# Another order of the same tasks in a fused recurrence and channel-mix kernel

## The chip, the cores and the metric

The kernel runs on one core of one Trainium2 chip. The metric is the device time of one execution in microseconds (us), as the median of three runs. A core has five engines with an instruction stream each: PE (matmul, with weight loads shown apart as PEld), DVE, ACT, POOL and SP, and 16 DMA engines that all queues share.

## The reference

A gated linear recurrence over 4 batches, 8 heads, 768 tokens and head size 48, whose output, as 384 channels per token, goes through a channel mix with 1024 hidden units:

```python
f = 1 / (1 + exp(-f_logit))
for t in range(S):
    state = f[:, :, t, :, None] * state + einsum('bhd,bhe->bhde', k[:, :, t], v[:, :, t])
    y[:, :, t] = einsum('bhd,bhde->bhe', q[:, :, t], state)
x = y.transpose(0, 2, 1, 3).reshape(B, S, H * D)
x_prev = concatenate([zeros((B, 1, D)), x[:, :-1, :]], axis=1)
xk = mu_k * x + (1 - mu_k) * x_prev
xr = mu_r * x + (1 - mu_r) * x_prev
k = maximum(xk @ w_k, 0)
return 1 / (1 + exp(-(xr @ w_r))) * (k * k @ w_v)
```

## The kernel before

**Work.** The recurrence is cut into 24 chunks i of 128 tokens (6 for each batch), the channel mix into 8 units u of 384 tokens (3 chunks). The mix's products are made as three products of high and low parts each (hi·hi, hi·lo, lo·hi), so that each weight and each operand is split in two by DVE, ACT and POOL.

**Tasks.** All work is cut into named tasks. For chunk i: loads `f`/`qk`/`v`; logarithms `zT`, `ez`, `ln`, `b`, `rb`, `e`; `q`, `kr`, `n`, `k`; `TR` or `QT` (transposes on PE) and `kt` (their copy, L363); `SP` (scores at L373 and sums at L393, on PE); `za`, `zb`, `T` (the state; `zb` is L330 or L333 on DVE); `YA`, `YB` (outputs, L410, on PE); `w`, `y` (copies), `bl` (L279) and `m` (the masked scores, L385). From chunk 8 on, `QT` `YA` `SP` `YB` of neighbouring chunks stand together as one bundle of small matmuls between the large ones. For unit u: `sp` (copies by DMA), `d`, `xm`, `xh`, `xl` (the mixed input and its two parts; `xh` is L544), `F` (L558, 9 matmuls each, input layer), `r`, `h`, `kk`, `l` (square and its parts), `R` (gate), `lg`, `sg` (sigmoid), `W` (output layer), `o` (L648, DVE), `out` (L652, the store; the last one goes out on ACT's queue, the others on SP's). The weights come in pieces: load, `S` L678, `T` L687, `X` L690 (all on DVE), `H` L693, `L` L697. `c`, `cm`, `lo`, `lot`, `lom` look at the inputs' sizes and set a flag, which `strong` (L802) reads into a register of every engine; at the end L887 branches around a general version of the whole program:

```python
at = U - 1
pl.add("lom", at, ("V", 0.6, 0, flag), uses=[("pm", "lo"), ("xm", "lo")])
pl.add("strong", at + 0.3, ("Q", 0.0, 0, load), after=["lom"])
...
k.emit(plan.schedule())
with tc.If(k.strong > 0):
    general(k, gen, out)
```

With the inputs timed here the flag is 0, the branch is taken on every engine, and the general code is skipped.

**What sets the order.** Two tables written out in full. `ORDER` lists every task once; `Plan.schedule` walks through it, a suffix (`:V` DVE, `:A` ACT, `:G` POOL) chooses the engine of a task, a token such as `+4y` puts four dummy matmuls (fillers, which keep PE running) there, and `HOMES` gives the buffer numbers. `Rwkv.emit` pins each engine's instructions to that order. So every engine works through its own part of `ORDER` strictly in turn, and waits where something that it needs from another engine or a DMA isn't there.

Of the kernel before, what the change touches and what calls it, by code (L numbers as in the profile page):

```python
# [63 lines left out]
+2m1 YA4 m4 d0.01 xh0.00:A xh0.02:A xm0.01 wvS3 xh0.01:V wvT3 wvX3 TR5 w4:A +1s YB4 kt5:A SP5 bl5:A wvH0 d0.12 za5:G
xl0.00:G xl0.02:G xl0.01:G d0.11 wvH3 wkH6 y4:A wvL0:G wkL6:G wvL3:G wkS5 F0.0 xm0.12 xm0.11 zb5 wkT5 wkX5 wkS7 wkT7 wkX7
F0.1 F0.2 YA5 F0.3 r0.0:A kk0.0:A d0.10 r0.1:A h0.0 h0.1 xm0.10 kk0.1:V m5 wv4 v8 v6 f3 wv5 b6 wvS4 wvT4 wvX4 r0.2:A l0.0:G
l0.1:G w5:A wkH5 YB5 kk0.2:A wkL5:G wrL3:G h0.2 ln6 rb6 r0.3:A kk0.3:A F0.4 F0.5 F0.6 r0.4:A wrH1 wkH7 h0.3 kr6:G l0.2:G
kk0.4:A r0.5:A h0.4 bl6:V q6 n6 k6 xh0.10:V xh0.12:V l0.3:V xh0.11:V xl0.10:V xl0.12:V TR6 kt6:A wkL7:G wrL1:G x01 F0.7 SP6
h0.5 kk0.5:A xl0.11:G l0.4:G l0.5:G r0.7:A y5:A wvH4 wvS5 wvT5 wvX5 r0.6:V kk0.6:V kk0.7:V h0.6 wvH5 R0.0 R0.1 R0.2 lg0.0:A
h0.7 b7 bl7:V m6 l0.7:V ln7 rb7 wvL4:G qk8 sp1.1 sp1.2 v7 sp1.0 l0.6:G wvL5:G kr7:G lg0.2:A lg0.1:A sg0 W0.00 W0.01 W0.10  # L70
W0.11 q7 n7 d1.1 k7 xm1.01 xm1.11 b8 d1.0 xm1.10 o0.0 xm1.00 ln8 rb8 bl8:A TR7 W0.20 W0.21 xh1.00:A kt7:A xh1.01:A xh1.10:A
xh1.11:A sf3 zb6:V T6 q8 kr8:G n8 k8 d1.2 out0.0 c5 qk9 xl1.00:G xl1.01:G xm1.02 xh1.02:A g7 xm1.12 o0.2 b9 QT8 YA6 w6:A SP7
YB6 ln9 rb9 xh1.12:A xl1.02:G za7:G xl1.10:G xl1.11:G kr9:G y6:A x02 g8 m7 q9 o0.1 F1.0 F1.1 F1.2 kt8:A qk10 zb7 bl9:V T7 n9
k9 za8:V b10 SP8 QT9 YA7 r1.0:A kk1.0:A h1.0 r1.2:A w7:A bl10:A ln10 rb10 kk1.2:V l1.0:G g9 m8 r1.1:V q10 zb8 kr10:G T8 n10
k10 h1.1 h1.2 kk1.1:A l1.2:V F1.3 YB7 v9 f4 qk11 out0.1 F1.4 F1.5 y7:A kt9:A b11 QT10 YA8 w8:V SP9 YB8 r1.4:A kk1.4:A h1.4
ln11 rb11 r1.5:V q11 bl11:V n11 l1.1:V za9:G xl1.12:G l1.4:G g10 g11 kr11:G k11 h1.5 kk1.5:A y8:A r1.3:A kk1.3:V l1.5:G h1.3
F1.6 F1.7 R1.0 R1.1 r1.6:V h1.6 r1.7:V h1.7 lg1.0:A kk1.6:A R1.2 l1.3:V kt10:V zb9 T9 m9 kk1.7:A za10:V cm5 lg1.1:A QT11 YA9
# [10 lines left out]
QT15 YA13 w13:V xl3.02:V SP14 YB13 za14:G bl16:A ln16 xh3.10:A rb16 kr16:G q16 cm2 n16 o2.2 zb14 k16 T14 m14 F3.0 F3.1 F3.2
F3.3 y13:A r3.0:A kk3.0:A h3.0 r3.1:A h3.1 kt15:A b17 xh3.12:V kk3.1:V v16 qk17 g15 l3.0:G za15:G xl3.10:V xl3.12:G l3.1:G
g16 QT16 YA14 w14:V SP15 YB14 r3.2:V r3.3:A xh3.11:A xl3.11:G ln17 rb17 kk3.3:A h3.3 h3.2 kk3.2:A zb15 bl17:V q17 y14:V F3.4  # L90
F3.5 F3.6 n17 l3.3:V m15 r3.5:V kr17:V kt16:V T15 k17 l3.2:G r3.4:A h3.4 kk3.4:A kk3.5:A h3.5 l3.4:G x04 l3.5:G r3.6:V F3.7
# [10 lines left out]
W4.11 W4.20 W4.21 v20 c9 out3.1 qk21 qk22 sf7 b21 ln21 bl21:A rb21 o4.0 out4.0 c13 b22 xh5.02:A ln22 rb22 bl22:A kr21:G q21
n21 k21 QT21 YA19 SP20 w19:A YB19 q22 o4.1 xl5.02:G g21 kr22:G kt21:A o4.2 xh5.11:V n22 k22 m20 b23 xh5.12:V zb20 T20 F5.0
F5.1 F5.2 r5.0:A y19:A h5.0 ln23 r5.1:V h5.1 QT22 YA20 kk5.0:V w20:V xl5.10:G xl5.11:G bl23:V cm13 cm9 l5.0:G SP21 YB20 v23
out4.2 qk23 out4.1 v22 rb23 r5.2:A kk5.1:A h5.2 y20:A kr23:G l5.1:G c8 sp6.0 sp6.2 q23 kk5.2:V F5.3 r5.3:A h5.3 kk5.3:A
l5.3:V l5.2:V n23 k23 kt22:V F5.4 F5.5 F5.6 r5.4:A h5.4 kk5.4:A g22 za21:G xl5.12:G g23 l5.4:G x06 r5.6:V m21 r5.5:V zb21
# [903 lines left out]
```

## Time and profile before

| | |
|---|---|
| time, median of 3 runs | 341.58 us (341.3 to 341.67) |
| time of the profiled execution | 341.73 us |
| its span, first to last instruction | 339.9 us |
| busy: PE, PEld, DVE, ACT, POOL | 320.8, 304.5, 255.5, 205.2, 153.4 us |
| matmuls | 4574 |
| moved by DMA | 45.24 MB |

Busy time is the sum of an engine's instructions as the profile shows them. The span's first part, up to the first `F` task (F0.0), is the start: loads, logarithms, weight pieces and the first chunks. The steady part follows, and the tail after the last matmul. PE's instructions are counted for the text as matmuls; each matmul has a weight load beside it, so 128 matmuls are 256 instructions, less a few waits that stand as instructions of their own.

### The profile page before, as it was taken

Reading aid. Unit: us, or ns where it says so; the run is one execution under the profiler, and the core shown is the slowest. Engines: PE = TensorE matmul, PEld = TensorE weight load, DVE = VectorE, ACT = ScalarE, POOL = GpSimd, SP = SyncE. Lnnn points to the kernel's source line nnn. Section 1 sums busy time; section 2 is a strip of 40 time slices with the busy share of each in tenths; the row PEclk is TensorE's granted clock in tenths of the full one; section 3 lists DMA queues with packets and bytes.
Section 4 is the critical chain, followed back from the end, with each engine's and each line's share of the span. In section 5 each row is a group of like instructions: output and inputs, shape, how many; then the busy total and the mean of one; then the engine's idle time right before and its main releaser. Section 6 shows DMA issues by size and latency. Waiting matters only on the chain. (4 is left out here: it accounts for less than half of the span.)

```text
span 339.9 us, 10992 instructions
## 1 busy us (share of the span) xinstructions
PE 320.8 (94%) x4574; PEld 304.5 (90%) x4574; DVE 255.5 (75%) x519; ACT 205.2 (60%) x432; POOL 153.4 (45%) x194
## 2 busy tenths in 40 slices
PE   4795889999999999999999999999999999999993
PEld 4675678899999999999999999999999999999993
DVE  5997999999988987686998886787475627837420
ACT  3888788784887736783658648591858236133420
POOL 2369589847762435313653356525612405214300
PEclk9999999999999999999999999999999999999999
DMA  7999667015465234470257122541520133040002
GB/s 230 398 385 360 185 193 273 14 29 158 175 198 152 75 97 153 102 267 25 87 125 269 62 46 85 170 143 60 187 91 5 32 117 92 35 141 23 0 4 79
DMA packets 20347, 45.24 MB, mean 133 GB/s; under 512 B 2752, under 2 KB 12736, under 8 KB 20288
## 3 DMA queue, kind: packets, MB, share of 16 engines
q1 hardware_dynamic: 20144, 44.25, 39.4%
q8 instruction: 38, 0.62, 0.8%
q10 hardware_dynamic: 144, 0.20, 0.2%
q14 instruction: 21, 0.17, 0.2%
HBM read 38.54 MB, written 4.72 MB: 127 GB/s over the span
## 5 line engine op out<-in xcount | busy, mean ns | idle before, releaser
L558 PE MATMUL pm<-xh,wk 128*128 128x384 f32 x384 | 103.5, 341 | 0.7 <-DVE words L690 0.5
L558 PE MATMUL pm<-wv,k2h 128*128 128x384 f32 x384 | 98.4, 338 | 0.0
L596 POOL TENSOR_TENSOR k2l<-kk,k2h 128x384 fp32r<-128x384 f32 x44 | 46.4, 1059 | 63.6 <-DVE kk L588 24.9
L558 PEld LDWEIGHTS pm<-xh,wk 128*128 128x128 f32 x384 | 69.8, 188 | 2.3 <-DVE words L690 0.6
L558 PEld LDWEIGHTS pm<-wv,k2h 128*128 128x128 f32 x384 | 69.0, 188 | 0.9 <-issue 0.5
L558 PE MATMUL pm<-wv,k2l 128*128 128x384 f32 x192 | 64.5, 336 | 0.4 <-issue 0.4
L558 PE MATMUL pm<-xl,wk 128*128 128x384 f32 x192 | 64.5, 336 | 0.0
L550 POOL TENSOR_TENSOR xl<-xm,xh 128x384 fp32r<-128x384 f32 x35 | 37.4, 1075 | 32.2 <-DVE xh L544 27.8
L289 POOL TENSOR_TENSOR qk<-qk,rb 128x256 f32<-128x256 f32 x23 | 17.1, 742 | 60.6 <-ACT rb L275 33.1
L586 ACT ACTIVATE k2h<-r 128x384 fp32r<-128x384 f32 x64 | 32.2, 519 | 12.8 <-DVE r L582 12.4
L558 PE MATMUL pm<-wr,xh 128*128 128x384 f32 x144 | 37.1, 339 | 0.3 <-DVE words L690 0.3
L558 PEld LDWEIGHTS pm<-wv,k2l 128*128 128x128 f32 x192 | 36.1, 188 | 0.0
L558 PEld LDWEIGHTS pm<-xl,wk 128*128 128x128 f32 x192 | 36.0, 188 | 0.0
L581 ACT ACTIVATE r<-pm 128x384 f32<-128x384 f32 x41 | 20.0, 488 | 24.5 <-PE pm L558 22.2
L558 PEld LDWEIGHTS pm<-wr,xh 128*128 128x128 f32 x144 | 25.8, 188 | 0.8 <-DVE words L690 0.6
L443 ACT ACTIVATE x<-py 64x128 f32<-64x128 f32 (+1 forms) x69 | 21.4, 310 | 8.1 <-PE py L410 4.9
L535 DVE SCALAR_TENSOR_TENSOR xm<-pm,mu_sb,x 128x384 f32<-128x384 f32 x42 | 24.9, 609 | 0.6
L270 DVE TENSOR_TENSOR_SCAN pm<-f,low 128x512 f32<-128x512 f32 x18 | 25.0, 1387 | 0.5 <-ACT f L624 0.3
L590 ACT ACTIVATE kk<-r 128x384 f32<-128x384 f32 x38 | 19.4, 519 | 9.6 <-DVE r L582 7.1
L558 PE MATMUL pm<-wr,xl 128*128 128x384 f32 x72 | 24.2, 336 | 0.0
L410 PE MATMUL py<-qk,z 64*64 64x64 f32 x704 | 21.6, 227 | 1.7 <-DVE z L330 0.9
L582 DVE TENSOR_SCALAR r<-pm 128x384 f32<-128x384 f32 x23 | 12.4, 549 | 12.8 <-PE pm L558 12.1
(129 smaller groups left out, 575.6 us busy)
## 6 DMA issues: line engine op xcount, KB each, us to landing
qk<-in_qkt SPq DMA_DIRECT2D x24, 512.0 KB, 5.6
...
v<-in_vt SPq DMA_DIRECT2D x24, 192.0 KB, 2.9
out<-o SPq DMA_DIRECT2D x23, 192.0 KB, 3.4
...
```

The lines of the kernel that those rows point to most:

```text
L270: pl.add(f"b{i}", ga, ("V", 1.25, 1, lambda: nc.vector.tensor_tensor_scan(b().rearrange(FL), f().rearrange(FL), self.low.rearrange(FL), 1. ...
L289: e.tensor_tensor(k()[:, ::2], k()[:, ::2], rb()[:, ::2], op=ALU.mult)
L410: first[c, h] = nc.tensor.matmul(to, lhs, rhs, start=(c, h) not in first, stop=stop, skip_group_check=True)
L443: e.activation(o, i_, AF.Copy, scale=sign)
L535: pl.add(f"xm{u}.{n}{j}", pr, ("V", 0.62, 0, lambda xm=xm, n=n, j=j: nc.vector.scalar_tensor_tensor(xm(), pm("d", u, j)[:, :UT], self.mu_s ...
L550: e.tensor_tensor(lo(), xm(), hi().bitcast(F32), op=ALU.subtract)
L558: nc.tensor.matmul(ps, lhs(a, j), rhs(bb, j), start=ends[0] and i == 0, stop=ends[1] and i == len(pr) - 1)
L581: pl.add(f"r{u}.{f}", kf, ("A", 0.5, 0, lambda r=r, ps=ps: nc.scalar.activation(r(), ps(), AF.Relu)), ("V", 0.56, 0, lambda r=r, ps=ps: nc ...
L582: ("V", 0.56, 0, lambda r=r, ps=ps: nc.vector.tensor_scalar(r(), ps(), 0.0, None, op0=ALU.max)),
L586: pl.add(f"h{u}.{f}", kf, ("A", 0.53, 0, lambda r=r, hi=hi: nc.scalar.activation(hi(), r(), AF.Square)), after=[f"r{u}.{f}"], **kw)
L590: ("A", 0.53, 0, lambda r=r, kk=kk: nc.scalar.activation(kk(), r(), AF.Square)),
L596: e.tensor_tensor(lo(), kk(), hi().bitcast(F32), op=ALU.subtract)
```

## The change

`ORDER` and `HOMES` are other tables; no task, no helper and no other line differs. The diff replaces all of both; here is its beginning and its end:

```diff
 ORDER = """
-f0.0 sf0.0 cst zT0 ez0 ln0 +2y b0 wr2 wrS2 wrT2 wrX2 wk2 wr0 wkS2 wrS0 f0.1 f0.2 sf0.1 wrT0 wkT2 sf0.2 wrX0 wkX2 wrH2 rb0
...
-TR3 w2:V YB2 e4 rb5 wrH3 bl4:A kt3:A wkH4 y2:A T2 wvS2 wvT2 wvX2 wrL2:G wkL3:G wkL2:G za3:G wkL4:G wkL0:G v3 SP3 x00 wk1 f2
...
-out6.1 c12 out6.2 lg7.0:A h7.7 l7.7:G W7.01 cm14 cm12 lg7.1:A lo lot W7.10 W7.11 lom strong lg7.2:V sg7 o7.0 out7.0 o7.1
-out7.1 W7.20 W7.21 o7.2 out7.2
...
+q3 T2 wvS2 +1m0 YA2 kr3:G x00 kr4:G wkL2:G za3:G TR3 w2:A wkH4 e4 kt3:A YB2 y2:A b5 SP3 wvT2 onemu wvX2 q4 bl4:V wvH2 rb5 e5
+wvS0 wvT0 f2 wr1 v4 zb3 T3 m3 TR4 kt4:A +4y SP4 YA3 wrS1 bl5:V wrT1 wrX1 wvX0 w3:V wk1 sf2 wvH0 m4 wkS1 wkT1 qk5 za4:G wkX1
...
+l7.5:G cm3 R7.2 W7.00 lo lg7.1:V lot lg7.2:A l7.6:G out6.0 sg7 kk7.7:V l7.7:G W7.01 W7.10 W7.11 W7.20 W7.21 o7.1 out7.1 o7.0
+o7.2 lom out7.2 strong out7.0
```

**DVE in the start, around `zb3` (L330, which waits for SP3's sums on PE).** Before, the piece `wvX2` (the first L690) and one more weight instruction stand ahead of it; `m` is L385, `T` is L336, `q` is L281:

```order
L678 TENSOR_SCALAR pm_94<-words_123 128x512
L687 SCALAR_TENSOR_TENSOR pm_94<-words_123,pm_94 128x512
L690 SCALAR_TENSOR_TENSOR words_123<-words_123,pm_94 128x512
L678 TENSOR_SCALAR pm_96<-words_k2h_131 128x384
L330 TENSOR_TENSOR z_77<-pss,z_76 128x4x48
L385 TENSOR_TENSOR ss_100<-pss,mask 128x512
L336 TENSOR_TENSOR sm<-pss,z_77 128x192
```

After the change the same place reads:

```order
L678 TENSOR_SCALAR pm_96<-words_123 128x512
L687 SCALAR_TENSOR_TENSOR pm_96<-words_123,pm_96 128x512
L775 TENSOR_SCALAR one_mu<-mu_sb 128x6
L690 SCALAR_TENSOR_TENSOR words_123<-words_123,pm_96 128x512
L281 TENSOR_TENSOR qk_64<-qk_64,pm_95 128x512
L279 COPY bl<-pm_95 128x4
L678 TENSOR_SCALAR pm_93<-words_122 128x512
L687 SCALAR_TENSOR_TENSOR pm_93<-words_122,pm_93 128x512
L330 TENSOR_TENSOR z_77<-pss,z_76 128x4x48
L336 TENSOR_TENSOR sm<-pss,z_77 128x192
L385 TENSOR_TENSOR ss_100<-pss,mask 128x512
```

`q4`, `bl4`, `wvS0` and `wvT0` have moved ahead of `zb3`.

**PE in unit 1, around the bundle of chunks 8 and 9.** Before, SP8 (L373, L393), QT9 (L351) and the first part of the L410 group (YA7) follow F1.2, the nine matmuls of F1.3 stand in between, and YB7 comes behind them:

```order
L373 MATMUL pss<-qk_64 64x64 x16
L393 MATMUL pss<-v_103,ktk_101 48x48 x16
L351 MATMUL py<-ident,qk_65 128x64 x8
L410 MATMUL py<-qk_67,z_77 64x64
L410 MATMUL py<-qk_67,z_76 64x64 x2
...
L558 MATMUL pm_96<-xh_124,wk_83 128x384
L558 MATMUL pm_96<-xl_125,wk_83 128x384
...
L410 MATMUL py<-qk_67,z_76 64x64
L410 MATMUL py<-ss_100,v_104 48x64 x16
```

After the change it is one bundle, directly behind F1.1 (the last of whose nine matmuls is the first row):

```order
L558 MATMUL pm_96<-xh_124,wk_84 128x384
L351 MATMUL py<-ident,qk_65 128x64 x8
L410 MATMUL py<-qk_67,z_77 64x64
L410 MATMUL py<-qk_67,z_76 64x64 x2
...
L373 MATMUL pss<-qk_64 64x64 x16
L393 MATMUL pss<-v_105,ktk_101 48x48 x16
L410 MATMUL py<-qk_67,z_76 64x64
...
L410 MATMUL py<-ss_100,v_104 48x64 x16
L558 MATMUL pm_93<-xh_124,wk_83 128x384
```

All 136 small matmuls of the bundle now stand together, one F task earlier.

**The end on SP.** The flag is loaded at L802; the `out` rows are stores of the last unit. Before:

```order
L652 DMA out<-o_119 128x384
L802 TENSOR_LOAD flag
L802 ISA x2
L652 DMA out<-o_120 128x384
L652 DMA out<-o_119 128x384
L887 COMPARE_AND_BRANCH
```

After:

```order
L652 DMA out<-o_120 128x384
L652 DMA out<-o_119 128x384
L802 TENSOR_LOAD flag
L802 ISA x2
L652 DMA out<-o_120 128x384
L887 COMPARE_AND_BRANCH
```

The load now has one store behind it instead of two. On DVE the four small instructions that make the flag (L795 to L798) have moved behind the last `o` (L648) and stand directly ahead of the branch:

```order
L648 TENSOR_TENSOR o_119<-pm_94,lg_121 128x384
L648 TENSOR_TENSOR o_120<-pm_93,lg_121 128x384
L648 TENSOR_TENSOR o_119<-pm_96,lg_121 128x384
L795 TENSOR_REDUCE xm_114<-pm_95 1x1
L796 TENSOR_REDUCE xm_114<-pm_95 1x1
L797 TENSOR_SCALAR xm_114<-xm_114 1x1
L798 SCALAR_TENSOR_TENSOR flag<-xm_114 1x1
L802 TENSOR_LOAD flag
L887 COMPARE_AND_BRANCH
```

Before, L795 to L802 stood ahead of `lg7.2` (L616) and of all three L648 rows.

## Rows read from the trace of the kernel before

**Rows 1.** Windows: length, busy (x instructions) of PE, PEld, DVE, ACT, POOL; clock; DMA; GB/s

```profile
27.25:33.45 6.20, 3.82 (x127) 3.27 (x126) 4.41 (x10) 4.73 (x13) 5.93 (x9) 1.00 0.94 366
45.50:81.90 36.40, 35.44 (x379) 33.43 (x381) 35.48 (x63) 27.86 (x58) 27.24 (x28) 1.00 0.38 124
45.50:112.40 66.90, 65.56 (x1016) 61.70 (x1017) 63.26 (x119) 51.09 (x108) 43.72 (x50) 1.00 0.45 144
112.40:334.40 222.00, 221.90 (x2830) 215.74 (x2829) 154.02 (x319) 119.96 (x252) 84.89 (x102) 1.00 0.30 95
```

**Rows 2.** Timeline of PE, its stops: start, duration, instruction, idle before

```profile
27.25 0.34 PE L373 MATMUL pss<-qk 64*64 64x64 f32 x8 [0.98 <-issue]
33.45 0.51 PE L373 MATMUL pss<-qk 64*64 64x64 f32 x19 [2.38 <-issue]
45.50 0.48 PE L410 MATMUL py<-ss,v 64*48 64x64 f32 x18 [0.58 <-issue]
47.16 0.44 PE L558 MATMUL pm<-xh,wk 128*128 128x384 f32 x1 [0.48 <-DVE words L690]
112.42 0.34 PE L558 MATMUL pm<-wv,k2l 128*128 128x384 f32 x1 [0.40 <-issue]
```

**Rows 3.** Waits in the start, 0 to 48 us: total, times, longest

```profile
DVE z L330 <- POOL qk L290: 2.0, 1, 2.0
DVE z L330 <- PE pss L393: 0.8, 1, 0.8
```

**Rows 4.** Windows of the start, columns as in group 1

```profile
9.00:35.00 26.00, 20.42 (x514) 16.78 (x515) 22.25 (x50) 22.16 (x51) 17.03 (x23) 1.00 0.97 368
35.00:47.20 12.20, 9.91 (x268) 7.90 (x267) 11.99 (x23) 9.12 (x21) 7.42 (x10) 1.00 0.69 220
```

**Rows 5.** Timeline of DVE in the start, single instructions

```profile
13.46 0.55 DVE L363 COPY ktk<-pm 128x384 f32<-128x384 f32 x1
16.57 0.35 DVE L333 COPY z<-pss 128x192 f32<-128x192 f32 x1
44.60 1.18 DVE L544 CAST xh<-xm 128x384 fp32r<-128x384 f32 x1
```

**Rows 6.** DMA view at 43.1, 82.0 and 110.1 us: packets, MB, busy share

```profile
q8 instruction: 1, 0.02, 60.3%
q8 instruction: 1, 0.02, 59.2%
q8 instruction: 1, 0.02, 60.4%
```

**Rows 7.** Windows, one bundle (QT11, YA9, SP10, YB9), columns as in group 1

```profile
107.01:109.31 2.30, 2.30 (x137) 2.15 (x136) 1.20 (x3) 2.16 (x3) 0.08 (x1) 1.00 0.72 223
```

**Rows 8.** Timeline of the end: the flag, the last output and its store

```profile
326.10 0.25 DVE L795 TENSOR_REDUCE xm<-pm 1x1 f32<-1x96 f32 x1 [5.79 <-PE pm L791]
326.64 0.15 DVE L798 SCALAR_TENSOR_TENSOR flag<-xm 1x1 int32<-1x1 f32 x1
334.92 0.56 DVE L648 TENSOR_TENSOR o<-pm,lg 128x384 f32<-128x384 f32 x1 [3.31 <-SPq L887]
335.51 0.38 ACTq L652 DMA_DIRECT2D out<-o  x1
```

**Rows 9.** SP's load of line 802: duration ns min/median/max, first and last start

```profile
L802 SPq TENSOR_LOAD <-flag x1: 477/477/477, 326.8 to 326.8; - x1
```

**Rows 10.** Instructions of line 887 on SP, columns as in group 9

```profile
L887 SPq EVENT_SEMAPHORE  x8: 17/17/17, 334.7 to 338.5; - x8
...
L887 SPq COMPARE_BRANCH  x1: 45/45/45, 332.0 to 332.0; - x1
```

**Rows 11.** Instructions of line 1006, columns as in group 9

```profile
L1006 SPq EVENT_SEMAPHORE  x10: 17/28/28, 338.6 to 339.9; - x10
```

**Rows 12.** DMA view 325 to 340 us: issues, KB each, us to landing

```profile
out<-o SPq DMA_DIRECT2D x2, 192.0 KB, 3.6
out<-o ACTq DMA_DIRECT2D x1, 192.0 KB, 2.7
```

More of the change, by code (lines that the diff above doesn't have):

```diff
@@ L60 @@
-e3 wkH3 w1:A bl3:A kt2:A m1 wrS3 wrT3 wrX3 T1 YB1 SP2 wk6 qk3 wv2 za2:G kr3:G wkH0 rb4 y1:A wkS6 wkT6 wkX6 zb2 m2 q3 b5 YA2
-TR3 w2:V YB2 e4 rb5 wrH3 bl4:A kt3:A wkH4 y2:A T2 wvS2 wvT2 wvX2 wrL2:G wkL3:G wkL2:G za3:G wkL4:G wkL0:G v3 SP3 x00 wk1 f2
-qk4 kr4:G wkS1 wv0 zb3 m3 T3 wkT1 wkX1 +1m1 YA3 +2s TR4 wr1 v4 qk5 wvH2 e5 sf2 w3:A wkH1 kt4:A q4 wvS0 wvT0 wrS1 wrT1 wrX1
-wvX0 q5 +4s YB3 wvL2:G za4:G kr5:G wkL1:G sp0.2 sp0.0 v5 sp0.1 d0.02 wv3 qk6 wk5 qk7 wk7 d0.00 xm0.02 y3:A xm0.00 SP4 zb4 T4
@@ L64 @@
[L64 to L77, printed above, removed]
@@ L88 @@
[L88 to L91, printed above, removed]
@@ L102 @@
[L102 to L106, printed above, removed]
@@ L117 @@
[L117 to L119 removed]
+cst f0.2 sf0.2 zT2 ez2 ln2 f0.0 sf0.0 zT0 ez0 ln0 f0.1 sf0.1 +1y zT1 wr2 wv1 wrS2 wrT2 wrX2 wrH2 ez1 ln1 b0 rb0 e0 wr0 qk0
+v0 wk2 qk1 wk0 wvS1 wvT1 wrS0 wrT0 wrX0 wvX1 b1 b2 wrH0 wvH1 kr0:G bl0:V q0 wkS2 wkT2 wkX2 rb1 e1 TR0 kt0:A +2y SP0 rb2 wkH2
@@ new lines @@
+e2 kr1:G TR1 f1 q1 wkS0 wkT0 wkX0 sf1 wk6 v1 zb0:A YA0 m0 bl1:A kt1:A zT3 T0 bl2:A w0:A wkH0 wkS6 wkT6 wkX6 mg0 wvL1:G za1:G
+zT5 SP1 YB0 ez3 ln3 ez5 y0:A wr3 qk2 wrS3 wrT3 m1 wrX3 zb1 T1 q2 wk3 v2 wk4 zT4 b3 YA1 w1:V kr2:G wrL0:G wkH6 wkL0:G wkL6:G
+za2:G TR2 YB1 ez4 ln4 kt2:A rb3 e3 wkS3 wkT3 wkX3 SP2 qk3 wkH3 y1:A b4 ln5 rb4 wkS4 wkT4 wkX4 zb2 m2 wv2 qk4 mu v3 wv0 bl3:V
+q3 T2 wvS2 +1m0 YA2 kr3:G x00 kr4:G wkL2:G za3:G TR3 w2:A wkH4 e4 kt3:A YB2 y2:A b5 SP3 wvT2 onemu wvX2 q4 bl4:V wvH2 rb5 e5
@@ new lines @@
+wvS0 wvT0 f2 wr1 v4 zb3 T3 m3 TR4 kt4:A +4y SP4 YA3 wrS1 bl5:V wrT1 wrX1 wvX0 w3:V wk1 sf2 wvH0 m4 wkS1 wkT1 qk5 za4:G wkX1
+zb4 q5 +1m2 YB3 wkL3:G wrL2:G wvL2:G sp0.0 d0.00 xm0.00 T4 xh0.00:V kr5:G wkL4:G wvL0:G y3:A TR5 sp0.1 sp0.2 d0.01 v5 wk7
+wv3 wk5 qk6 xm0.01 d0.02 wrH3 kt5:A YA4 w4:A +1m2 +2s SP5 YB4 xh0.01:A d0.11 xm0.02 wkS7 wkT7 wkX7 xm0.11 wvS3 wvT3 wvX3
+xh0.02:A d0.10 wkH1 wkH7 d0.12 y4:A wvH3 za5:G xl0.00:G xl0.01:G xl0.02:G x01 wkL1:G wrL3:G wvL3:G F0.0 F0.1 xm0.12 zb5
+xm0.10 wkS5 wkT5 wkX5 F0.2 YA5 F0.3 r0.0:A h0.0 kk0.0:A r0.1:A h0.1 kk0.1:A r0.2:A w5:A m5 b6 wv4 wv5 qk7 qk8 f3 v6 wkH5 YB5
@@ new lines @@
+xl1.00:G ln9 T6 q8 n8 k8 d1.2 xm1.02 xh1.10:A xh1.01:A rb9 xh1.02:A QT8 YA6 SP7 w6:A YB6 y6:A kt8:A bl9:V o0.1 q9 n9
+xl1.01:G g7 za7:V xl1.02:G g8 kr9:G zb7 T7 xm1.12 k9 m7 F1.0 F1.1 out0.0 c8 v10 qk10 b10 QT9 YA7 w7:V SP8 YB7 xh1.11:A
+r1.0:A h1.0 kk1.0:A ln10 rb10 bl10:A xh1.12:A za8:G xl1.10:G r1.1:V zb8 T8 o0.2 l1.0:G kr10:G m8 q10 n10 k10 kk1.1:A h1.1
+kt9:V l1.1:G F1.2 F1.3 r1.3:V F1.4 F1.5 y7:A r1.2:A kk1.2:A h1.2 r1.4:A h1.3 kk1.3:A b11 ln11 rb11 QT10 YA8 l1.2:V w8:V
+out0.2 v9 qk11 SP9 YB8 f4 v11 out0.1 l1.3:V xl1.12:G xl1.11:G g9 za9:G x02 h1.4 kk1.4:V l1.4:G kr11:G r1.5:A kk1.5:V kt10:V
```

96 lines of the change are left out of this document (54 added, 42 removed).

## The prediction

> **What bounds the kernel now.** I read the windows first, then what PE waits for, then DVE in the start, then the end. The windows [rows 1] show a PE that does not rest: from 112.40 to 334.40 it is busy 221.90 of 222.00 us, from 45.50 to 112.40 it is busy 65.56 of 66.90, and the granted clock is 1.00 in every row, which is the higher of the two levels. DVE is busy 154 of 222 us there and nothing waits for it long. So the time is three parts: how late PE comes to the first F task (F0.0, 47.16 us, [rows 2]), the steady matmuls, the same products in both kernels, and what follows the last matmul. Only waits that PE meets on the way can lengthen the middle part.
>
> PE's own stops are the next thing to see [rows 2]: 0.98 us before 27.25, 2.38 before 33.45, 0.58 before 45.50, 0.40 before 112.42. All four say "issue": no engine was waited for. They stand at fixed counts: 127 matmuls lie between the first two and 1016 = 8 x 127 between the last two [rows 1], that is 256 instructions with the weight loads. And in the DMA view an instruction packet of 16 KB on queue q8 starts 2.4 us before PE goes on at 45.50, at 43.1, and 2.3 us before 112.42, at 110.1 [rows 6]. I read this as PE's instructions being fetched in blocks of 256: a block is asked for some time after PE enters the one ahead of it, is there 2.35 us after its packet starts, and PE stops if it gets through a block sooner. The delay up to the packet varies. The three blocks from 45.50 on end at 81.9 (381 weight loads, [rows 1]) and the packet starts at 82.0, 0.1 us later. The block ahead of 112.42 begins inside the bundle of [rows 7], at 107.6 by counting back 127 matmuls, and its packet starts at 110.1, 2.5 us later. Over the 28 blocks from 45.50 on the middle delay is 0.7 us.
>
> DVE in the start is nearly full: 22.25 of 26.00 us, then 11.99 of 12.20 [rows 4]. Its two long waits are 2.0 and 0.8 us, both ahead of L330 (`zb3`, `zb2`) [rows 3]. The 2.0 is put down to POOL, whose instruction had ended long before; what came last were SP3's sums on PE, inside which the stop of 2.38 us stands. The 0.8 is the same with SP2 and the stop of 0.98. The transfers are heavy to 35 us too (share 0.97).
>
> **The change, part 1: the start.** I counted DVE's work in its order up to the last instruction that F0.0 needs. Before, that is `xh0.01`, with 75 tasks of 39.9 us in all. After, it is `xm0.02` with 73 tasks, 37.5 us by the same durations. Left out are `kt0` 0.55 and `zb0` 0.35, now on ACT, the 1.18 of `xh0.01` (stretched; its like take about 0.4) [rows 5], `wvS3`, `w0`, `w2` and two `bl`; five small copies and one `xh` come in. So 2.4 us go. Then the waits: the order shows `q4`, `bl4`, `wvS0` and `wvT0`, some 2.5 us by their durations, now ahead of `zb3`. They run while SP3 stands still, so at most the 2.0 us of [rows 3] are filled too. Together 4.4 us could go, but ACT carries the copies (22.16 of 26 us, hardly freer than DVE, [rows 4]), the transfers set when weights are there, and a stop just ahead of SP4 is possible (below). Walking through the new order by hand with these durations puts F0.0 at 43.5 to 45 us; I take 44.3, **-2.9**. Bounds: -1.2, half of the work that goes and no wait filled, and -4.2, nearly everything. Two fillers fewer (14 to 12) are in the walk. The DVE work between F0.0 and later F and R tasks is equal within 0.5 us, so I see nothing that takes this gain back in unit 0.
>
> **Part 2: the blocks of 256.** In the steady part the order of the matmuls moves where blocks end. Large matmuls take about 0.34 us busy each but one starts every 0.17 us, a block of them lasts 22 us; a bundle of 136 small ones takes 2.30 us [rows 7], so a block that falls on one bundle whole is through in little over 2 us. Before, the nearest pair of block ends is 3.6 us apart and passes without a stop; the only steady stop, 0.40, has 4.8 us but the latest packet of all. After, counting through the order: one block begins at the seventh matmul of F1.1, just ahead of the bundle in the order shown, and ends inside YB7, 2.4 us later; one runs from the end of F3.2 into YB14, 2.1 us; one from YA20 into F5.4, 2.2 us. W1.01 meets an end as before, 4.6 us. With a delay of 0.65 and 2.35 to arrive, a block needs 3.0 us: stops of 0.6, 0.9 and 0.8, together **+2.3**. Bounds: with no delay, or a block asked for ahead, +0.2; with the longest delay seen, 2.5 us, each stop is 2.5 to 2.8 and W1.01's is kept, and not all three can be the worst, so +5. I take the middle delay, since [rows 6] has both short and long ones. Joining SP8 and YB7 to one bundle saves a change between small and large matmuls, **-0.1**.
>
> The Trainium skill speaks against this term. "Runtime: NRT & Kernel Launch", section "Instruction fetch mechanics", also has refills in 16 KiB blocks of 256 instructions, but says that the cost of crossing is mostly hidden; by that the term would be 0 and the sum -1.0, 340.7 us. The four stops of [rows 2] do not agree with "hidden" for dense small matmuls, and the measurement decides.
>
> **Part 3: the tail.** Before, the flag is made from 326.10 to 326.79 [rows 8], 7 us ahead of the end; SP's load takes 0.477 [rows 9] and lies beside the last matmuls. SP's branch, taken, starts at 332.0 and its next instruction runs at 334.7 [rows 10]: 2.7 us to fetch the code behind the skipped part, hidden too. What ends last is the store of ACT, issued at 335.51 [rows 8], landing 2.7 later [rows 12], and ACT's own branch; then SP's events run from 338.6 to 339.9 [rows 11]. After, the order shows the four flag instructions behind the last `o`, which ends at 335.48 before [rows 8]. Counted on that clock: 0.69 for the flag, 336.2; SP's load 0.48, 336.7, and some 0.5 to move and check it; a store `out7.0` (0.4 to issue) that stands behind the load; the branch at 337.4; 2.7 to the next code, 340.1; then about the 1.3 us of [rows 11] and the eight events ahead of them [rows 10], some 0.5: 341.9. The store alone gives nearly the same: issued at 337.3, 2.7 to 3.6 to land [rows 12], and about 1.2 behind it, 341.2 to 342.1. Against 339.9 I take **+2.0**, bounds +1.4 (events overlap the landing) and +2.8 (both late and one after the other). What is queued behind the flag's load is each engine's branch; DVE's and ACT's (both ready by 337) end before SP's.
>
> By the skill's same section a taken branch to code outside the loaded window forces a fetch; the trace agrees, 2.7 us on SP.
>
> **Sum.** -2.9 + 2.3 - 0.1 + 2.0 = +1.3. The profiled execution took 341.73 us, 1.83 beyond its span of 339.9; it stands 0.15 above the median of the runs. Against the median 341.58 the sum gives **342.9 us**. A measurement of this kernel can tell about 0.2%, 0.7 us, from no change.
>
> **Rivals.**
> - *The blocks come in time* (other side). The mechanism is the same queue, but packets start as at 82.0, right at the crossing, and a block is there when the bundle ends; the stops add up to 0.2. Then -2.9 + 0.2 - 0.1 + 2.0 = -0.8, 340.8 us. For it: every steady block but one passed without a stop in the trace. Against it: none was shorter than 3.6 us, and a packet needs 2.35. It decides for faster where the three stops stay under 0.3 us in all. Chance 0.22; a start of -4.2 with stops of 1.2 together (-1.1, 340.5) ends on the same side and adds 0.03.
> - *The start's gain is absorbed.* SP4 now holds a block end only 3.9 us after the one in SP3, in the time when transfers are densest and packets come latest (3.5 us after the crossing for the one at 43.1); a stop of 2 us there, with `zb4` and what follows on DVE waiting for it as `zb3` did, leaves -0.5 to -1 of the start: -0.8 + 2.3 - 0.1 + 2.0 = +3.4, 345.0. For it: two of the four stops stood in just such places. Against it: DVE has other work ahead of most of its waits now. Chance 0.15.
> - *The terms cancel.* Stops of 0.3 to 1.5 us, or a start nearer -4, land within 0.7 us of before: 341.6. Chance 0.22.
> - *The forecast*, +0.7 to +2.6: 0.38.
>
> That the change does not do what it says is no rival: each engine's order is pinned.
>
> **Numbers.** Faster 0.25 (first rival and the large start), same 0.22, slower 0.53 (forecast and absorbed start). The range leaves out the fastest tenth (stops of nothing with a start beyond -3.4) and the slowest tenth: 340.3 to 344.9. The forecast alone covers 342.3 to 344.2.
>
> **What would show it.** F0.0 between 43.5 and 45 us shows part 1 right; 46 or later with an "issue" stop in SP4 shows the absorbed start. PE stops marked "issue" of 0.3 us or more inside YB7, YB14 and F5.4 show part 2 right, a steady part without them the first rival. The flag made behind the last `o`, SP's branch as the last long wait and 7 to 8 us from the last matmul to the end, against 5.6 before, show part 3. I am wrong if DVE or a transfer holds PE somewhere in the steady part, where I saw the same work in another order and took it as covered, or if the granted clock falls below 1.00.

## The result and the profile after

The changed kernel takes 346.0 us (median of 4 runs, 344.12 to 348.07); before, beside it, takes 341.62. The ratio is 1.0139, with a 95% interval of 1.0106 to 1.0172: slower by 3.6 to 5.9 us. It lies above the forecast of 342.9 and above its range. The second comparison of the same kernel (e1 below) gave 1.0097 (1.0064 to 1.013), 3.3 us; the four runs of the first were on the late side. In three of the kernels below (e4, e8, e10) one execution took 400 to 1079 us, which nothing here explains; the ratios do not contain them.

The profiled execution took 344.12 us, span 342.4. The windows, cut at F0.0 (47.94) and at the second R task of unit 0 (R0.1, 65.77), ahead of which PE waits for DVE for 0.2 to 0.3 us in all four profiles of the two kernels; columns as in [rows 1]:

```profile
9.00:47.94 38.94, 32.10 (x776) 26.31 (x775) 35.22 (x73) 32.46 (x72) 26.92 (x34) 0.91 0.86 309
47.94:65.77 17.83, 17.61 (x221) 16.31 (x213) 16.61 (x30) 15.41 (x38) 16.75 (x16) 1.00 0.45 159
65.77:334.40 268.63, 268.35 (x3565) 260.42 (x3565) 190.81 (x394) 156.42 (x320) 111.48 (x138) 1.00 0.33 103
```

PE is full behind R0.1, as it was. But F0.0 comes at 47.94 where it was 47.16 [rows 2], not at 44.3, and the clock, 1.00 in all rows before, is 0.91 in the start. The stops and waits of PE, timeline as in [rows 2], the last row of the steady part:

```profile
34.44 0.51 PE L373 MATMUL pss<-qk 64*64 64x64 f32 x19 [2.06 <-issue]
40.67 0.33 PE L344 MATMUL pm<-ident,qk 128*128 128x128 f32 x1 [0.29 <-POOL qk L289]
41.36 0.55 PE L344 MATMUL pm<-ident,qk 128*128 128x128 f32 x3 [0.36 <-POOL qk L290]
42.97 0.46 PE L410 MATMUL py<-qk,z 64*64 64x64 f32 x16 [1.06 <-ACT stage L443]
90.17 0.38 PE L410 MATMUL py<-ss,v 64*48 64x64 f32 x10 [0.23 <-issue]
```

The stop inside SP3 is there again. Two new waits stand behind it, on POOL (`kr5`, ahead of TR5) and on ACT (`y3`, ahead of YA4). The stop inside YB7 is exactly where it was forecast, but it is 0.23 us and not 0.6; inside YB14 and F5.4 there is none. And SP4's block end, which the absorbed-start rival named, passes without a stop.

The end, timeline and then lines 802, 887 and 1006 on SP, with PE's branch (PEldq), columns as in [rows 8] and [rows 9]:

```profile
334.01 0.34 PE L558 MATMUL pm<-wv,k2l 128*128 128x384 f32 x1
334.38 0.56 DVE L648 TENSOR_TENSOR o<-pm,lg 128x384 f32<-128x384 f32 x1 [3.08 <-PE pm L558]
334.86 0.23 DVE L795 TENSOR_REDUCE xm<-pm 1x1 f32<-1x96 f32 x1
335.39 0.15 DVE L798 SCALAR_TENSOR_TENSOR flag<-xm 1x1 int32<-1x1 f32 x1
336.69 0.34 SPq L652 DMA_DIRECT2D out<-o  x1
```

```profile
L802 SPq TENSOR_LOAD <-flag x1: 730/730/730, 335.6 to 335.6; - x1
L887 SPq EVENT_SEMAPHORE  x8: 17/17/17, 340.3 to 341.0; - x8
...
L887 PEldq COMPARE_BRANCH  x1: 4356/4356/4356, 336.5 to 336.5; - x1
...
L887 SPq COMPARE_BRANCH  x1: 45/45/45, 337.1 to 337.1; - x1
...
L887 PEldq EVENT_SEMAPHORE  x1: 51/51/51, 340.9 to 340.9; - x1
L1006 SPq EVENT_SEMAPHORE  x10: 17/28/28, 341.1 to 342.3; - x10
```

The last matmul starts at 334.01, 0.03 us later than before (333.98), and the end is 8.39 us behind its start; before it was 5.93. This distance is called the tail below. So this execution has the whole difference of the spans (2.5 us) in the tail: start +0.78, F0.0 to the last matmul -0.75, tail +2.46. The other executions have more than that, and the experiments look for it in the start.

### The profile page after: what moved, and what is told of

The parts are those of the page before. It is cut to its first block, busy times and chain, and to the rows that moved or that the text cites. A ratio compares the mean times of both kernels' runs of the same rounds, so it can differ in the third digit from the quotient of the medians.

```text
span 342.4 us, 10993 instructions
## 1 busy us (share of the span) xinstructions
PE 322.8 (94%) x4570; PEld 307.1 (90%) x4570; DVE 249.1 (73%) x512; ACT 208.7 (61%) x434; POOL 156.9 (46%) x199
## 4 chain that ended last, share of the span: by engine, by line
PE 83%; DVE 5%; POOL 4%; DMA 3%; issue 2%; SPq 2%; ACT 0%; POOLq 0%; DVEq 0%
PE pm L558 67%; PE py L410 7%; PE pss L373 3%; DMA f<-in_zt 3%; PE pss L393 2%; PE py L351 2%; POOL k2l L596 1%; PE pm L252 1%; DVE xm L530 1%; SPq L684 1%; POOL xl L550 1%; PE pm L258 1%; DVE pm L270 1%; DVE pm L687 1%; PE pm L344 0%
## 5 line engine op out<-in xcount | busy, mean ns | idle before, releaser
L596 POOL TENSOR_TENSOR k2l<-kk,k2h 128x384 fp32r<-128x384 f32 x44 | 47.4, 1085 | 74.7 <-ACT k2h L586 33.6
L550 POOL TENSOR_TENSOR xl<-xm,xh 128x384 fp32r<-128x384 f32 x39 | 42.7, 1106 | 40.9 <-DVE xh L544 24.1
L581 ACT ACTIVATE r<-pm 128x384 f32<-128x384 f32 x46 | 22.5, 489 | 22.0 <-PE pm L558 20.2
L270 DVE TENSOR_TENSOR_SCAN pm<-f,low 128x512 f32<-128x512 f32 x18 | 27.0, 1508 | 1.4 <-ACT r L581 1.1
L648 DVE TENSOR_TENSOR o<-pm,lg 128x384 f32<-128x384 f32 x24 | 12.9, 550 | 18.6 <-issue 9.1
L410 PE MATMUL py<-qk,z 64*64 64x64 f32 x704 | 21.7, 228 | 1.1 <-ACT stage L443 1.1
L590 ACT ACTIVATE kk<-r 128x384 f32<-128x384 f32 x32 | 16.7, 522 | 9.7 <-DVE r L582 6.6
```

The source lines that it names most:

```text
L270: pl.add(f"b{i}", ga, ("V", 1.25, 1, lambda: nc.vector.tensor_tensor_scan(b().rearrange(FL), f().rearrange(FL), self.low.rearrange(FL), 1. ...
L410: first[c, h] = nc.tensor.matmul(to, lhs, rhs, start=(c, h) not in first, stop=stop, skip_group_check=True)
L550: e.tensor_tensor(lo(), xm(), hi().bitcast(F32), op=ALU.subtract)
L581: pl.add(f"r{u}.{f}", kf, ("A", 0.5, 0, lambda r=r, ps=ps: nc.scalar.activation(r(), ps(), AF.Relu)), ("V", 0.56, 0, lambda r=r, ps=ps: nc ...
L590: ("A", 0.53, 0, lambda r=r, kk=kk: nc.scalar.activation(kk(), r(), AF.Square)),
L596: e.tensor_tensor(lo(), kk(), hi().bitcast(F32), op=ALU.subtract)
```

## The experiments

Ratios are against the kernel before, run on the same chip at the same time (its medians were 341.3 to 341.8). Each kernel left one profile. The times of one kernel scatter by 2 to 4 us, those of before too (339.84 to 343.94 over 91 executions), so that one profile is one draw. In e2, e3 and e4 the numbers of lines from 123 on are one lower.

**e1: the changed kernel again** (no edit).

> The changed kernel once more, for a second profile, since its four times lie between 344.1 and 348.1 us while those of before agree within 0.5. Start theory: the scatter comes from TensorE's clock and the instruction fetches in the start; F0.0 again at 47 us or later (47.9 in the first profile), the granted clock at 1.2 GHz for some stretch before it, and the later the time, the later F0.0. Steady theory: F0.0 at 47.9 +-0.3, and PE shows stops marked issue of 0.5 to 2.5 us inside YB7, YB14 or F5.4 where the first profile shows none.

344.87 us (344.04 to 346.45). F0.0 at 49.85, last matmul at 335.65, tail 8.53. Two rows of PE's timeline:

```profile
28.70 0.89 PE L393 MATMUL pss<-v,ktk 64*48 64x48 f32 x30 [3.50 <-issue]
44.99 0.71 PE L410 MATMUL py<-qk,z 64*64 64x64 f32 x16 [1.21 <-ACT stage L443]
```

This time the stop is in SP2, 3.50 us, and none in SP3. From F0.0 on nothing differs: 285.80 us to the last matmul against 286.07. The start theory holds, the steady theory falls. That before agrees within 0.5 us, as expected here from three times, does not hold over more of them.

**e2: the flag early again.**

```diff
-kk7.7:V l7.7:G W7.01 W7.10 W7.11 W7.20 W7.21 o7.1 out7.1 o7.0 o7.2 lom out7.2 strong out7.0
+kk7.7:V l7.7:G W7.01 lom strong W7.10 W7.11 W7.20 W7.21 o7.1 out7.1 o7.0 o7.2 out7.2 out7.0
```

> The changed kernel with the flag and its load (lom, strong) moved back ahead of the last W tasks and so ahead of the last outputs; nothing else differs. Tail theory: the distance from the last matmul to the end of the span falls from 8.1 us to about 5.6, so the time is 2.0 to 2.8 us less than that of the changed kernel run beside it (about 343.5 against 346). Rival, the stores' landing sets the end anyway: less than 0.5 us.

343.21 us (340.9 to 344.75), 1.0042 (1.0013 to 1.007). Against e1 that is 1.7 us less in the medians, somewhat under the 2.0 expected; the tail is 6.24 us. That the late flag costs time in the tail is settled: in the four profiles with a late flag (the changed kernel, e1, e3, e11) the tail is 8.1 to 8.5 us, in the thirteen with an early one 5.1 to 6.7. 1.4 us remain that are not in it. This profile is also the changed start with hardly a stop (0.40 us in SP3, none in SP2), and yet F0.0 is only at 46.58. Two rows of PE, and POOL's timeline up to F0.0:

```profile
46.58 0.44 PE L557 MATMUL pm<-xh,wk 128*128 128x384 f32 x1 [1.42 <-DVE xm L529]
89.97 0.38 PE L409 MATMUL py<-ss,v 64*48 64x64 f32 x10 [0.60 <-issue]
```

```profile
38.16 1.31 POOL L696 TENSOR_TENSOR wv<-words,wv 128x512 fp32r<-128x512 f32 x1
39.42 0.74 POOL L288 TENSOR_TENSOR qk<-qk,rb 128x256 f32<-128x256 f32 x1
40.10 0.74 POOL L289 TENSOR_TENSOR qk<-qk,rb 128x256 f32<-128x256 f32 x1
40.80 1.03 POOL L696 TENSOR_TENSOR wk<-words_k2h,wk 128x384 fp32r<-128x384 f32 x1
41.77 1.31 POOL L696 TENSOR_TENSOR wv<-words,wv 128x512 fp32r<-128x512 f32 x1
43.02 0.63 POOL L322 TENSOR_TENSOR z<-sm,bl 128x192 f32<-128x192 f32 x1
43.62 2.93 POOL L549 TENSOR_TENSOR xl<-xm,xh 128x384 fp32r<-128x384 f32 x3
```

POOL has no pause from 38.16 to 46.55, and F0.0 starts 0.03 us behind its last xl. The wait is put down to DVE, whose `xm0.02` had ended at 44.35. Low parts of weights and `kr5` stand ahead of the three xl.

**e3: the start of before, the rest of the changed kernel** (all tasks ahead of F0.3 in the order of before, 3 buffers renamed).

> The tasks ahead of F0.3 in the order of before (its engines, fillers and buffers there), then the changed kernel's order, its tail included. Start theory: PE reaches F0.0 at 47.2 us and never at the low clock, the scatter goes; steady part and tail as in the changed kernel, so 343.4 to 344.2 us, all runs within 0.6. Steady theory: scatter stays, 345 to 347 us.

346.92 us (345.66 to 347.45), 1.0146 (1.0116 to 1.0177). Both expectations fail: the scatter is small, but the time is no better. F0.0 is at 48.62, with stops of 1.25 and 2.66 us in SP2 and SP3, 7 us at the lower clock behind them, and PE waits 1.11 us ahead of YB5 and 0.92 ahead of R0.1, where the two kernels themselves wait for 0.3 us at the most. Whether the joint of the two orders or the renamed buffers made these waits was not tried, so that e3 gives no price for the start.

**e4 and e5: the changed start, the rest and the tail of before.** In both, the tables of the changed kernel stand ahead of F0.3 and those of before behind it, with five buffers renamed, v6 and v7 among them; in e5 buffers 1 and 2 of `v` are exchanged for all later chunks too, so that each load of `v` waits for the chunk for which it waits in before. The joint is not quite clean: five tasks that only the changed kernel has ahead of F0.3 (`d0.10`, `wkH7`, `x01`, `wrL3`, `xm0.10`) stay behind it, and `qk7` stays ahead of it.

> The reverse: the tasks ahead of F0.3 in the changed order, then the order of before, its tail included. Start theory: the scatter comes along with the start; 342.5 us at best and up to 346, F0.0 at 47.9 us or later. Steady theory: 342.3 to 342.8 us and all runs within 0.6.

> The changed order ahead of F0.3, then the order and tail of before, as in the run e4, but with the buffers of v from chunk 6 on renamed together, so that each load of v waits for the same chunk as before. If the 1.76 us wait of PE at R1.0 in e4 came from a load of v held up by a renamed buffer, it is gone, steady part 286.5 to 287.2 us, time 341.5 to 343.0. If it comes with the changed start itself, the wait stays and the time is 344 to 345 again.

e4: 344.69 us, 1.0066 (1.004 to 1.0093), F0.0 at 46.93, with a wait of 1.76 us at R1.0 and 3.4 us at the lower clock behind it; q11 on DVE and `kr11` on POOL both began late there. In e5 that wait is gone: 343.23 us (341.71 to 344.19), 1.0035 (1.0014 to 1.0056), steady part 285.82. So e4 was disturbed by its renamed buffers, and e5 shows the changed start nearly alone: 1.2 us slower than the start of before (0.5 to 1.9). F0.0 was at 50.21 in its profile, with this stop in SP2 and what it did on DVE (`zb2`):

```profile
29.14 0.89 PE L393 MATMUL pss<-v,ktk 64*48 64x48 f32 x30 [3.77 <-issue]
30.56 0.36 DVE L330 TENSOR_TENSOR z<-pss,z 128x192 f32<-128x192 f32 x1 [3.50 <-PE pss L393]
```

e5 and e2 differ in all that follows F0.3 and cost nearly the same (1.0035, 1.0042): the changed rest is worth about nothing, either way. The profiles agree: from R0.1 to the last matmul it is 267.9 to 268.5 us in before, e9, e11 and e15, and 268.0 to 268.6 in the changed kernel, e1 and e2.

**e6 and e10: less of POOL ahead of F0.0** (both on e2; e10 leaves wkL4 in place).

```diff
-... YB3 wkL3:G wrL2:G wvL2:G ... kr5:G wkL4:G wvL0:G ... xl0.02:G x01
+... YB3 wkL3:G wvL2:G ... kr5:G ... xl0.02:G wrL2:G wkL4:G wvL0:G x01
```

> The changed kernel with the early flag of e2, and three low parts of weights (wrL2, wkL4, wvL0, 3.2 us of POOL) moved behind the last xl of unit 0. Theory that POOL's queue holds F0.0 up (POOL is busy without a break from 38.2 to 46.5 us in e2, and F0.0 starts at 46.58): F0.0 at 45.5 to 46.3 us, where ACT's last xh and one subtraction end next, and 0.3 to 1 us less than e2 in runs at the same clock. Rival, DVE alone sets it: F0.0 stays at 46.6 or later and the time at 341 to 344.

> As e6, but wkL4 stays where it was and only wrL2 and wvL0 (2.1 us of POOL) stand behind the last xl of unit 0. POOL theory: the wait of 1.44 us for wkL4 ahead of F0.4 in e6 is gone, F0.0 about 0.5 us earlier than in e2 at equal stops (46.1 where SP2 and SP3 lose 0.4 us), time 0.3 to 0.6 us less than e2, so about 1.003 of before. Rival, the place of F0.0 doesn't reach the end: 1.004 or more of before.

e6 has the same stop in SP3 as e2 (0.40) and brings F0.0 to 45.73, 0.85 us earlier: POOL's queue did hold it. But PE then waits 1.44 us inside F0.1 for `wkL1`, which now stands behind what was moved (POOL has it from 48.92 to 49.92), and the time is 344.73, 1.0087 (1.0059 to 1.0115), not less than e2 but more. e10 was expected to be rid of that wait, which I had taken for one for wkL4; `wkL1` is late there too, the wait is 0.78 us, F0.0 at 46.80, and the time 343.73, 1.0062 (1.0031 to 1.0093), the number of the rival: an earlier F0.0 does not reach the end here. Rows of PE in e6, F0.0 and F0.1:

```profile
45.73 0.44 PE L558 MATMUL pm<-xh,wk 128*128 128x384 f32 x1 [0.69 <-DVE xm L530]
...
49.98 1.00 PE L558 MATMUL pm<-xh,wk 128*128 128x384 f32 x2 [1.44 <-POOL wk L697]
```

**e7: the gap ahead of zT3 filled** (on e2).

```diff
-kt1:A zT3
+kt1:A +8y zT3
```

> The changed kernel with the early flag of e2, and eight more dummy matmuls ahead of zT3, where PE stands still for 2.0 to 2.2 us in all profiles with this start. Theory that TensorE's clock falls behind such a gap: no stretch at 1.2 GHz between 19 and 23 us, and the mean granted clock of the runs rises by about 0.005. If that stretch costs time: F0.0 up to 1 us earlier and the median under that of e2 (343.2) by as much; if the other engines hide it: F0.0 and the time as in e2. The blocks of 256 shift by 16 too, so the 0.60 us stop inside YB7 should be gone.

Windows 18 to 24 us, in the changed kernel and then in e7:

```profile
18.00:24.00 6.00, 5.59 (x124) 5.28 (x124) 5.21 (x12) 3.41 (x9) 4.61 (x6) 0.72 1.06 393
```

```profile
18.00:24.00 6.00, 6.00 (x134) 5.42 (x133) 5.09 (x11) 3.18 (x9) 5.16 (x7) 1.00 1.06 390
```

The low clock is gone from there (it falls later, 0.58 of full from 42.90 to 47.00), and the mean clock of the executions is 0.992, as before's beside it, where e2 has 0.988. The time is 342.98, 1.0037 (1.0008 to 1.0065), like e2, so no gain shows. The profile had stops of 0.96 and 1.72 us in the start. The stop in YB7 is gone, as expected, but one of 1.51 us stands in the output layer of unit 1 instead, at 111.63.

**e8: the bundle of unit 1 split** (on e2): F1.1 between SP8 and YB7.

> The changed kernel with the early flag of e2, and F1.1 moved in between SP8 and YB7, so that the block of 256 that held the whole bundle holds nine large matmuls too and lasts 3.5 us or more instead of 2.7 to 3.3. Block theory: no stop marked issue inside YB7 (0.60 us in e2, 0.2 in the changed kernel), steady part 0.3 to 0.6 us shorter than in e2 for the same waits elsewhere, the median 0 to 0.6 us under that of e2. Rival: the stop stays inside YB7, wherever the block begins.

```profile
88.58 0.54 PE L393 MATMUL pss<-v,ktk 64*48 64x48 f32 x32
89.05 0.44 PE L558 MATMUL pm<-xh,wk 128*128 128x384 f32 x1
...
90.81 0.46 PE L410 MATMUL py<-qk,z 64*64 64x64 f32 x16
91.10 0.77 PE L410 MATMUL py<-ss,v 64*48 64x64 f32 x32
```

No stop in YB7: the block theory holds for the stop. The time expected from it does not show: the steady part is 287.14 us against 287.22 in e2, and from R0.1 to the last matmul it is 268.51 where e1, with the bundle whole and without a stop, has 267.96. The time, 344.71, 1.0078 (1.0048 to 1.0108), tells nothing of 0.6 us: its start had stops of 1.11 and 2.33 and F0.0 at 48.06.

**e9: before again.**

> The kernel before once more, for a second profile of its start. Over eight profiles of the changed start F0.0 stands at 45.7 to 50.2 us and follows the stops marked issue inside SP2 and SP3 nearly one for one. Theory that the start of before hides these stops better: F0.0 between 45.5 and 47.5 us whatever they are (3.9 us of stops gave 47.16). Rival, that both starts take them alike and the first profiles were luck: F0.0 under 45 us where the stops are under 1 us, or over 48 where the low clock joins them.

Stops of 1.27 and 2.66 us, a stretch at the low clock behind them, F0.0 at 48.68, 342.59 us. The rival's "over 48 where the low clock joins" came true; stops that small did not occur in any profile with this start (3.4 to 3.9 us in SP2 and SP3 together). Its windows up to F0.0 and up to R0.1 (67.03):

```profile
9.00:48.68 39.68, 32.69 (x780) 27.18 (x780) 34.38 (x72) 31.65 (x71) 24.44 (x32) 0.96 0.85 310
48.68:67.03 18.35, 17.88 (x213) 16.29 (x213) 17.94 (x32) 15.14 (x37) 16.29 (x17) 1.00 0.44 152
```

**e11: the late flag put into before.**

```diff
-W7.11 lom strong lg7.2:V sg7 o7.0 out7.0 o7.1 out7.1 W7.20 W7.21 o7.2 out7.2
+W7.11 lg7.2:V sg7 o7.0 out7.0 o7.1 out7.1 W7.20 W7.21 o7.2 lom out7.2 strong
```

> The kernel before with the flag's four instructions and its load moved behind the last output, the stores as they were: the tail's suspected cost alone, put into the other kernel. Tail theory: 1.9 to 2.4 us more than before, about 343.7, the distance from the last matmul to the end 8.0 us or more against 5.9. Rival, that the late store out7.0 of the changed kernel made its tail long, which is left out here: less than 1 us.

343.8 us (342.94 to 344.9), 1.0073 (1.0051 to 1.0095), 2.5 us more; tail 8.12. The late flag costs this by itself, without the late store. SP's branch and its next instruction:

```profile
L887 SPq EVENT_SEMAPHORE  x8: 17/17/17, 340.2 to 340.7; - x8
...
L887 SPq COMPARE_BRANCH  x1: 45/45/45, 336.6 to 336.6; - x1
```

**e12: what helped, together** (e5 with the POOL move of e10 and the filled gap of e7).

> What the runs so far point to together: the changed start with wrL2 and wvL0 behind the last xl of unit 0 and with eight dummy matmuls in the gap ahead of zT3, then the order and the tail of before. If the start's loss is POOL's queue and the low clock: 340.3 to 341.5 us, as good as before or better, and no stretch at the low clock near 20 us. If the loss is the stops inside SP2 and SP3 alone: 342 to 343.5 us with a scatter of 3 us, F0.0 following them.

343.1 us (341.65 to 345.89), 1.0059 (1.0035 to 1.0083): no better than e5, and the second expectation's time, though that one goes by stops in SP2 and SP3, and this profile, of the fastest execution, has none there. F0.0 47.25, a stop of 1.14 us in the start, no low clock near 20 us but one stretch from 42 to 46. The mean clock of the executions is 0.993, as before's beside it: the lower clock by itself is not what the changed start loses.

**e13, e14, e15: a large load taken out of the time of the stops** (e13 and e14 on e2, e15 on before; e14 moves the sigmoid further back too).

```diff
-... f2 ... qk5 ...
+... qk5 f2 sf2 ...
```

> The changed kernel with the early flag of e2, and the load f2 (768 KB, first used behind F0.3) issued behind qk5 instead of five loads earlier, which takes it out of the time in which the instruction blocks inside SP2 and SP3 are fetched. Theory that the stops there are fetches held up by transfers: the stop inside SP2 (0 to 3.8 us in the profiles of this start) is 0, the scatter of the times shrinks from 4 to about 2 us, and the median falls to 341.5 to 342.5. Rival, the fetch is late for another reason: the stop and the scatter stay, the median stays at 343 or above.

> As e13, and the sigmoid sf2 of that load, 4 us of ACT with its two table loads, moved behind the last xh of unit 0 that stands on ACT. Theory that ACT's queue makes PE wait for y3 (1.0 to 1.6 us before YA4 in these profiles) and so holds F0.0 up beside POOL: that wait is gone, F0.0 under 46.2 us at small stops; whether it reaches the end shows at R0.0, 65.2 us in e2 at the earliest. Rival, DVE sets R0.0: F0.0 earlier, R0.0 still at 65 us or later and no time gained.

> The kernel before with the same load f2 and its sigmoid behind qk5. Transfers theory: the stops inside SP2 and SP3, 1.0 to 1.3 and 2.4 to 2.7 us in four profiles, become smaller by 1 us or more together, F0.0 comes under 47 us, and the time is 0.3 to 1 us under that of before. Rival: the stops stay as they are, time within 0.3 us of before.

e13: 344.73, 1.0109 (1.0074 to 1.0144); e14: 348.41, 1.0207 (1.0151 to 1.0263); e15: 341.93, 1.0026 (1.0006 to 1.0046), 0.9 us more and so neither expectation's time. The stops stayed in all three (1.27 and 2.38 us in e15), here in e13, which also waited 3.51 us ahead of YA4:

```profile
27.79 0.57 PE L393 MATMUL pss<-v,ktk 64*48 64x48 f32 x30 [1.58 <-issue]
35.49 0.51 PE L373 MATMUL pss<-qk 64*64 64x64 f32 x19 [2.33 <-issue]
```

So this load is not what holds the blocks up, and the theory falls as far as this load goes. In e14 the wait for `y3` shrank to 0.75 us, but PE stopped for 3.98 us in SP3 and then waited 2.06 for a weight part at F0.1 that ACT now made late. ACT had no room either. (The 65.2 us that e14's text gives to R0.0 is R0.1's time.)

## Why the prediction was wrong, step by step

**The start: wrong sign, and the step that failed.** The forecast was -2.9, from "walking through the new order by hand ... puts F0.0 at 43.5 to 45 us". The best profile of the unmodified start has 46.58, the six of them 46.58 to 50.21, and e5 prices the start at +1.2 us. Three things were wrong in that step.

First, the work that was to go did not go. The walk counts 2.4 us less of DVE up to the last instruction that F0.0 needs. DVE's busy time from the first instruction of the span to the end of that one, in before, in the changed kernel and in e2 (window, its length, busy and number of instructions of DVE, clock, DMA share, GB/s):

```profile
0.00:45.78 45.78, 37.95 (x83) 1.00 0.88 312
0.00:44.80 44.80, 37.53 (x81) 0.95 0.84 296
0.00:44.35 44.35, 38.20 (x81) 0.96 0.87 301
```

That is 0.4 us less in the changed kernel and 0.2 more in e2. One reason: the `xh` that comes in on DVE is stretched as `xh0.01` was, 0.79 us and 1.09 in e2. That it ends at 44.35 in e2, inside the range walked for F0.0, is luck: PE stopped for 0.40 us in SP2 and SP3 there, and for 3.36 in the trace that the walk started from.

Second, the walk followed DVE to that instruction and stopped there. But the mixed input then goes through ACT (`xh0.02`) and POOL (`xl0.02`), and POOL's queue, which the argument looked at nowhere, was 8.4 us deep without a pause in e2. Freeing it moved F0.0 by 0.85 us (e6), and what came next was full too: POOL's part of the next weights (e6, e10) and ACT (e14). In the changed kernel's own profile POOL's last xl ends at 47.16, and F0.0 comes 0.78 us later still, without a wait: PE, at the lower clock from 43.8 to 47.2, is only then through with YB4. So it is in e1, e5, e7 and e12, by 0.6 to 0.8 us. A clock below 1.00 was a sign of being wrong that the prediction named. This last part is caught up by R0.1: from F0.0 to there these five profiles take 17.8 to 18.4 us, and e2, e4 and e8, where PE waits for POOL, 18.6 to 18.8.

Third, the place of F0.0 does not set the time. DVE is full up to 81.90, which [rows 1] showed (35.48 of 36.40), and PE waits for it again ahead of R0.1. From 9 us to R0.1 DVE is busy 51.9 to 52.3 us in the four profiles with the start of before (before, e9, e11, e15) and 51.8 to 52.9 in the changed kernel, e1, e2 and e8, and R0.1 comes at 65.77 where it was 65.53 to 67.03 in those four. The prediction's count behind F0.0, equal within 0.5 us, held: from that last instruction on DVE is busy 19.3 us up to R0.1 in before and 19.5 to 19.7 in these four. What was not there is the 2.4 us ahead of it. POOL shows that an early F0.0 alone is worth nothing: in e6 it is 0.85 us earlier than in e2, and R0.1 comes at 67.08 against 65.20.

**The covered wait was only partly covered.** Filling the 2.0 us at `zb3` with four tasks was part of the -2.9. In the changed kernel DVE still waits 1.01 us there, behind a stop of 2.06; in e1 and e5 the stop was in SP2 (3.50, 3.77), where `zb2` has nothing more behind which to hide it (3.50 idle on DVE in e5). By the profiles the changed start takes the stops in SP2 and SP3 worse (us; the third column is the time at the lower clock that follows them directly):

| start, profile | stops in SP2 and SP3 | lower clock behind them | R0.1 |
|---|---|---|---|
| of before: before | 3.36 | 0 | 65.53 |
| e11 | 3.66 | 0 | 65.80 |
| e15 | 3.65 | 3.4 | 65.98 |
| e9 | 3.93 | 3.4 | 67.03 |
| changed: e2 | 0.40 | 0 | 65.20 |
| e4 | 0.67 | 0 | 65.69 |
| changed kernel | 2.52 | 0 | 65.77 |
| e8 | 3.44 | 3.4 | 66.69 |
| e1 | 3.50 | 6.8 | 67.69 |
| e5 | 3.77 | 6.8 | 68.22 |

How much of the difference is the clock's, no run separates. The executions point the same way: the seven of e2 with a mean clock of 0.987 or less took 343.2 to 344.8 us, the five with 0.990 or more 340.9 to 341.8. Of before the 18 with 0.988 or less have a median of 342.5, the 57 with 0.992 or more 341.1. But e7 and e12 raised the mean clock and gained nothing, so that it may only mark the executions with long stops. Why the stops are longer at one time than at another stays open; no kernel tried here took them away for certain.

**The steady part: the right places, the wrong size.** The term was +2.3 for three blocks. Measured: 0.23 us in YB7 (0.60 in e2), nothing to be seen in the two others. Two terms were mis-sized. One is the delay of the packet, taken as 0.65 us behind the entry of the block. PE entered the block of YB14 at 166.55 and its successor's packet starts at 166.30, 0.25 us ahead, and the block took 2.1 us as counted; for the block of F5.4 the packet starts 1.4 us ahead of the entry. The trace of before already had this: PE entered one block at 165.96 whose successor's packet starts at 165.11, and one at 308.12, behind 22 us of large matmuls, whose successor's packet starts 2.9 us ahead. A middle value over all blocks hid it. The other is the length of a block: the one of YB7 took 2.7 us without its stop and the one of F5.4 2.9, where 2.4 and 2.2 were counted; YB7's delay was 0.56, near the forecast's. So the rival "the blocks come in time" was right here. That the changed rest is worth about nothing follows from e2 beside e5.

The Trainium skill's "mostly hidden" ("Runtime: NRT & Kernel Launch", section "Instruction fetch mechanics") is thus a fair word for most blocks of the steady part, with stops of 0.4 us at the most in the two kernels' profiles, but 0.60 in e2 and 1.51 in e7. It is not one for the start, where every profile had stops, 0.4 us in all at the least and 4 us at the most in SP2 and SP3. The sum that the prediction gives by that rule is 340.6 us by its own terms, not 340.7.

**The tail: right.** Forecast +2.0, bounds 1.4 to 2.8. Measured +2.46 between the profiles, 1.7 by taking it out (e2 against e1), 2.5 by putting it in (e11). Of its steps, the flag took 0.68 us as said; SP's load 0.73 instead of 0.48, and 3.2 us went from SP's branch to its next instruction, not 2.7. What came back last from the branch in this profile was PE, at 340.9, 0.6 us behind SP (in e1 it was SP); the forecast looked at SP, DVE and ACT alone. From the end of the last matmul, which is how the prediction's 5.6 was counted, it is 8.05 us, at the upper edge of the 7 to 8 named as a sign. The late store adds 0.4 us at the most beside it: e11, without it, has a tail of 8.12.

**The -0.1** for one change between small and large matmuls is too small for these runs; e8, where the bundle is split again, hints at more (268.51 us from R0.1 on against 267.96 in e1), by one profile each.

**The sum.** Start +1.2 (e5), rest about +0.2, tail 1.7 to 2.5: 3.1 to 3.9, against 3.3 in e1 and 3.6 to 5.9 in the first comparison. Of the rivals the absorbed start came nearest (345.0), but by another mechanism: not SP4's block end, but DVE's work up to R0.1, POOL's queue, and stops in SP2 and SP3. The two misses lie on opposite sides: the start came out 4.1 us worse than forecast and the steady part 2.1 better, so that the measured time is nearer to the forecast than the start's error alone would put it, by luck. No version here beats before.
